# One ring for the probability tiles, a new order of attention's steps, and more decode steps inside the last heads

## The chip, the cores and the metric

The program runs on one core of a Trainium2 chip. The metric is device time in microseconds (us), median over runs of the whole program. TensorE (PE) does the matrix products, VectorE (DVE), ScalarE (ACT) and GpSimd (POOL) the element-wise work, and SyncE (SP) issues all DMA transfers.

## The reference

Sixteen heads of attention, then two feed-forward layers on their output, all checked at float32 accuracy:

```python
q_pool = q.reshape(B, H, S // 2, 2, D).mean(axis=3)          # B, H, S, D = 2, 8, 1152, 64
scores = scale * q_pool @ k.T;  scores -= scores.max(-1)     # per head: 576 queries x 1152 keys
attn = exp(scores) / (exp(scores).sum(-1) + 1e-9)
x = (attn @ v) -> (1152, 512)
x = ((x @ w_a) * (x @ w_b)) @ w_out                          # 512 -> 1536 -> 512, weights in float64
out = sum over 4 experts of p_e * (relu(x @ w1_e) @ w2_e)    # 512 -> 1024 -> 512
```

## The kernel before

Every float32 product is built from rounded parts ("hi" and "lo"), so most operands are first split by a cast on ScalarE and a difference on VectorE or GpSimd.

**Attention.** A head's scores come in nine tiles of 128 keys by 576 queries (a "qk": four matmuls, lines 570 and 575), each followed by an exponential on ScalarE (line 580) into a probability tile e. Each tile is used by a value product (pv, line 656) and, for the sum of each row, by VectorE adds (ad, line 593; on GpSimd for head 1) and products with ones (on, lines 612 and 600). The maximum of each row is needed ahead of the scores: maximum matmuls (mx, line 452) with a VectorE reduction each (lines 467 and 490), then a small transpose (rm) and a DMA into row 64 of QL (row_put). Heads go in pairs; while one pair's scores run, the next pair's Q and K are loaded, split and placed by DMAs (da, dh, dl) and casts (db). A finished pair is normalized: nr, nb (reciprocal of the sums and its spread), two n (product, split into X). Head 0 runs apart, in two parts of its queries (tokens A and C for scores, a and c for value products, x and y for maxima of heads 0 and 1).

**The order** of all of it is written out by hand as lists of such tokens. The loop at line 863 walks through them and issues what each stands for on its engine's queue; each engine runs its queue in order and waits by semaphores. FIRST is for heads 0 and 1, PROG1 for heads 2 and 3, PROG for each pair of heads 4 to 13, PROGZ for 14 and 15. A token that isn't ready may be skipped.

**Probability tiles** are 640 columns wide, eleven of them in a pool (NE = 11); ring() asserts that what lay in a place has been used up. Head 0's half tiles use 512 or 640 of the columns, the others 576.

**Gate and output products.** Weights of the first feed-forward layer come as float64. One gate block f (of 12) has 1 MB of them, loaded into one of two raw tiles (token sd, w_dma) and decoded by w_split_steps into WA, 1024 columns in two chunks of 512. decode64 does a chunk in seven stages with a stop (yield) behind each of the first six: copy on ScalarE (line 198), clamp, shift, or, cast to hi on ScalarE with a mask on VectorE (lines 216, 217), product, then lo (lines 230 and 231, with a subtraction on GpSimd, line 226). A token w runs the decode to its next stop:

```python
        def early_steps():
            yield from w_split_steps(late=False)
            yield from w_split_steps(0, 2 * pools["n"])
```

That is all of block 0's weights (WA0, 13 stops with the one at its end) and the first chunk of block 1's (WA1, 6 stops). What is left of it when attention has been issued is run behind the last pair's normalization, and then the third load:

```python
        for _ in early:
            pass
        while nxt["dma"] < 3:
            w_dma()
```

Then come block 0, whose products are ordered by tokens (first tokens 0 to 383 for all kc, then the others for kc 0 to 2, then kc 3, where the last pair's result lies), WA1's second chunk, blocks 1 to 11 with 72 matmuls each (line 1056), the weights of f + 1 being decoded beside block f, the output product (three groups of 108 in line 1056, the fourth in line 1280) and the experts (lines 1331 and 1403).

Of the kernel before, what the change touches and what calls it, by code (L numbers as in the profile page):

```python
# [7 lines left out]
F32 = mybir.dt.float32  # L8
# [9 lines left out]
SQ = S // 2  # L18
HQ = SQ // 2
KT = S // 128  # L20
# [15 lines left out]
KR = 3  # L36
KN = S // KR
WARM = (8, 4, 3)
NE = 11
NS = 4  # L40
CHAINS = ((0, 1, 2, 3), (4, 5, 6, 7), (8,))
QQ = HQ // 2
# [2 lines left out]
C1 = SQ - C0  # L45
FIRST = """
A
A x wu x
A x x x
A kh1 x  # L50
A x a qh1 a x kl1 a a a x r1 a dh1
C zq
C a c
C c c ql1 qs da1 qh k lv1 lq c klo0 y y
C y y ql y
C qb y lk0 a y y a y E1 y y dh y y y c y mx db1 c qs c R1 c mx mx c mx mx
qk mx dl mx
qk mx
qk mx mx
qk mx mx  # L60
qk mx mx lk2 E2
qk lk1 klo2 qh ldf mx
qk mx ad pv pv k ad pv mx ad klo1 on ad
qk ad db
qk mx pv pv ad pv mx da pv pv on rm qb
""".split()
FIRST_ONLY = set("A C a c x y r1 R1 E1 E2 qh1 kh1 kl1 ql1 da1 dh1 db1 lv1 zq wu".split())
PROG1 = """
on dh mx dn lq pv rw evac
qk  # L70
qk mx ad
qk pv
qk da mx klo0 dl ldf ad nr klo1
qk
qk nb pv mx
qk lk0 pv ad
qk ad mx
qk pv on ad db pv pv ql ad
qk mx
qk ad  # L80
qk on qs pv on qh
qk mx pv ad ad pv sd lk1 evac dn
qk
qk mx ad pv lk2 klo2 pv
qk mx
qk k da pv dl pv pv pv on pv qb n ad dh rm ad
qk db ldf n
""".split()
PROG = """
da klo0 mx pv klo2 pv on sd on pv dn evac  # L90
qk
qk mx
qk
qk pv dl ad ql pv mx
qk
qk dh ad pv pv klo1 rw lk0 lk2 ad mx db lk1 nr
qk ad pv lq ldf pv on mx ad
qk pv ad
qk
qk mx  # L100
qk pv on ad on dh mx dn
qk
qk pv evac qs ad qh
qk mx ad
qk ad pv pv pv k
qk nb mx pv dl db pv on pv da qb n rm
qk ad
qk n ad ldf
""".split()
PROGZ = """  # L110
pv rw pv da db
qk
qk on on ad pv w dn evac nr
qk w
qk pv pv pv
qk ad
qk pv pv ad dh w w
qk dl ad
qk pv w
qk  # L120
qk ad pv ad
qk
qk pv
qk
qk ad on w ad w ad on on
qk
qk pv nb ad ldf ad evac
qk n ad
qk dn n
""".split()  # L130
ENG = {"add1": "P", "klo1": "P", "ql1": "P", "qs1": "P", "klo2": "P", "ql2": "P", "qs2": "P", "add": "V", "qs": "V", "qh": "A", "k": "A", "ql": "V", "klo": "V", "mult": "V", "xhi": "A", "xlo": "V"}
F64_SCALE = 2.0 ** -112
# [4 lines left out]
def kernel(  # L137
# [118 lines left out]
    with tc.manual_schedule():  # L256
        att = ExitStack()
# [1 line left out]
        pair_p = att.enter_context(tc.tile_pool(name="pair", bufs=2))  # L259
        lo_p = att.enter_context(tc.tile_pool(name="lo", bufs=2))  # L260
        b_p = att.enter_context(tc.tile_pool(name="b", bufs=1))
        e_p = att.enter_context(tc.tile_pool(name="e", bufs=NE))
        m_p = att.enter_context(tc.tile_pool(name="m", bufs=2))
        u_p = att.enter_context(tc.tile_pool(name="u", bufs=2))
        r_p = att.enter_context(tc.tile_pool(name="r", bufs=1))
# [6 lines left out]
        pools["tmp"] = lambda i: [tmp_p.tile([128, 256], F32, tag=f"{x}{i}", name=x) for x in "vct"]  # L272
        ps_p = ctx.enter_context(tc.tile_pool(name="ps", bufs=1, space=PSUM))
        PS = ps_p.tile([128, 8, BANK], F32, name="PS")
        turn = {"s": 0, "mx": 0, "st": 0, "ps": 0, "po": 0}

        def psum(kind, base, n, count):
            i = turn[kind]
            turn[kind] = (i + 1) % count
            return PS[:, base + i * n:base + (i + 1) * n, :]  # L280
# [13 lines left out]
        def rows(i):  # L294
            return slice(64 * i, 64 * i + 64)
# [23 lines left out]
        E_t, U_t, D_t = ({} for _ in range(3))  # L319
# [214 lines left out]
        def qk_half(c, u):  # L534
            st = psum("st", 4, 2, 2)
            n, at = ((C0, 0), (C1, C0))[c]
            cs = slice(at, at + n)
            ts = [t for t in (2 * u, 2 * u + 1) if t < KT]
            for j, t in enumerate(ts):
                ks = slice(t * 128, (t + 1) * 128)  # L540
                nc.tensor.matmul(out=st[:, j, :n], lhsT=At[0][:, ks], rhs=QHt[0][:, cs], start=True, stop=False)
                nc.tensor.matmul(out=st[:, j, :n], lhsT=Bt[0][:, ks], rhs=QLt[0][:, cs], start=False, stop=True)
            e = e_p.tile([128, 2, C1], F32, tag="e", name="e")
            k = len(ts)
            nc.scalar.activation(out=e[:, :k, :n], in_=st[:, :k, :n], func=AF.Exp, scale=1.0 / 16.0)
            for j, t in enumerate(ts):
                halves_t[c, t] = e[:, j, :n]
# [8 lines left out]
        def evac_half(c):  # L556
# [5 lines left out]
            if c == 1:  # L562
                den_gather(0, 0, U_t[0][64:65])

        def qk(h, t):
            i = h % 2
            st = psum("st", 4, 2, 2)
            ks = slice(t * 128, (t + 1) * 128)
            for c in range(2):
                nc.tensor.matmul(  # L570
                    out=st[:, c, :HQ], lhsT=At[i][:, ks], rhs=QHt[i][:, c * HQ:(c + 1) * HQ],
                    start=True, stop=False,
                )
            for c in range(2):
                nc.tensor.matmul(  # L575
                    out=st[:, c, :HQ], lhsT=Bt[i][:, ks], rhs=QLt[i][:, c * HQ:(c + 1) * HQ],
                    start=False, stop=True,
                )
            e = E_t[h, t] = e_p.tile([128, 2, C1], F32, tag="e", name="e")[:, :, :HQ]
            nc.scalar.activation(out=e, in_=st[:, :, :HQ], func=AF.Exp, scale=1.0 / 16.0)  # L580

        S_t = {}
# [35 lines left out]
        e_ring = []  # L618

        def ring(new):  # L620
            if len(e_ring) >= NE:
                kind, a, t = e_ring[-NE]
                if kind == "half":
                    assert (a, t) not in halves_t and (a, t + 1) not in halves_t
                else:
                    assert kind == "full" and pv_at[0] > a * KT + t
                    c = [t in x for x in CHAINS].index(True)
                    if len(CHAINS[c]) > 1:
                        assert ad_at[0] > (a, ADDS.index((c, max(1, CHAINS[c].index(t)))))
                    else:  # L630
                        assert on_at[0] > (a, c)
            e_ring.append(new)

        def den(h):
            pr, o = divmod(h, 2)
            if pr == NH // 2 - 1:
                if o == 0:
                    ring(("D", 0, 0))
                    D_t[pr] = e_p.tile([128, 2, C1], F32, tag="e", name="e")[:, :, :HQ]
                for c in range(2):  # L640
                    nc.scalar.activation(
                        out=D_t[pr][rows(o), c, :], in_=PS[rows(c), 1, :HQ], func=AF.Copy, bias=1e-9
                    )
                return
            d = dn_p.tile([128, QQ], F32, tag="dn", name="dn")
            nc.scalar.activation(out=d, in_=PS[:, 0, HQ:HQ + QQ], func=AF.Copy)
            if o == 0:
                dc_t[pr] = m_p.tile([128, SQ // 64], F32, tag="dc", name="dc")
            nc.sync.dma_start(
                out=dc_t[pr][rows(o), :],  # L650
                in_=d.rearrange("(g r) n -> g r n", g=4)[:, 0, :].rearrange("g (p n) -> g p n", p=16),
            )
# [18 lines left out]
        def den_gather(pr, o, den):  # L671
            if o == 0:
                dc_t[pr] = m_p.tile([128, SQ // 64], F32, tag="dc", name="dc")
            nc.sync.dma_start(
                out=dc_t[pr][rows(o), :],
                in_=den.rearrange("o c n -> o (c n)").rearrange("o (p n) -> o p n", p=64),
            )
# [129 lines left out]
        def first(tok):  # L807
# [3 lines left out]
            if tok in "AC":  # L811
                assert tok == "A" or "r1" in emitted
                qk_half(tok == "C", n)
                emitted.update((tok, t) for t in (2 * n, 2 * n + 1))
                if tok == "C" and n == KT // 2:
# [47 lines left out]
        for h in range(1, min(NHX, NH)):  # L863
            s = -1
# [3 lines left out]
            half = ([i for i, t in enumerate(prog) if t == "qk"] + [0] * KT)[KT]  # L868
            for tok in prog if h == 1 else prog[half:] if h % 2 else prog[:half]:
# [8 lines left out]
                elif tok == "qk":  # L878
                    s += 1
                    assert ("row", h) in emitted and all((x, h) in emitted for x in "abhl")  # L880
                    if h == 1:
                        assert {"ql1", "db1", "da1", "dh1"} <= emitted
                    qk(h, s)
                    emitted.add(("qk", h, s))
                elif tok == "mx":
# [4 lines left out]
                elif tok == "rm":  # L890
                    if h + 1 < NH:
                        p = h // 2 + 1
# [9 lines left out]
                elif tok == "pv":  # L902
                    hh, j = divmod(pv_at[0], KT)
# [12 lines left out]
                elif tok == "ad":  # L916
                    hh, j = ad_at[0]
# [5 lines left out]
                elif tok == "on":  # L923
                    hh, j = on_at[0]
# [18 lines left out]
                elif tok in ("nr", "nb", "n"):  # L943
                    i = norm_at[0]
                    pr, i = divmod(i, 4)
# [12 lines left out]
                elif tok in ("lq", "lk0", "lk1", "lk2"):  # L958
                    p = nxt_ld[tok]
                    if p < NH // 2:  # L960
# [4 lines left out]
                        else:  # L965
                            r = int(tok[2])
# [12 lines left out]
                elif tok in ("da", "db", "dh", "dl"):  # L979
                    g = puts[tok[1]]  # L980
                    if g < NH and h > 0:
                        puts[tok[1]] += 1
                        p = g // 2
# [5 lines left out]
                elif tok in ("k", "qs", "qh", "qb"):  # L989
                    p = nxt_pre[tok]  # L990
# [48 lines left out]
        pr = NH // 2 - 1  # L1039
# [62 lines left out]
        w = W.pop(("ab", 0))  # L1102
# [22 lines left out]
        for f in range(1, NF):  # L1125
            if f == STOP:
                return
            w = W.pop(("ab", f))
# [26 lines left out]
        def o_w(d, hf):  # L1155
            while ("o", (d, hf)) not in W:
                next(ahead, None)
            w = W.pop(("o", (d, hf)))
            if d < KC - 1:
                for _ in range(9):  # L1160
                    if nxt["split"] < 15 + 2 * d + hf or splits[14 + 2 * d + hf][:2] not in W:
                        next(ahead, None)
                if (d, hf) == (KC - 2, 1):
                    for _ in ahead:
                        pass
            return w
# [64 lines left out]
        for d in range(KC - 1):  # L1231
            px2 = psum("ps", 0, NTC, 2)
            for hf in range(2):
                w = o_w(d, hf)
# [37 lines left out]
        w = [o_w(KC - 1, hf) for hf in range(2)]  # L1272
# [105 lines left out]
        for k in range(NP // 2):  # L1378
            e = k // 2
# [18 lines left out]
            for tt_i in (5, 6, 7, 8, 0, 1, 2, 3, 4):  # L1398
                po = psum("po", 6, 1, 2)[:, 0, :]
# [63 lines left out]
```

## Time and profile before

| | us |
|---|---|
| median of 3 runs | 864.03 (862.67 to 864.32) |
| the profiled execution | 862.54 |
| its span, first to last instruction | 860.7 |
| TensorE busy | 843.1 |
| VectorE busy | 638.1 |
| ScalarE busy | 338.4 |

The span is what the profile's rows cover; some 1.8 us lie around it. An engine's busy time counts its instructions' time; matmuls are pipelined and their ends are modelled, so a busy TensorE is not one at its peak.

### The profile page before, as it was taken

Reading aid. Unit: us, or ns where it says so; the run is one execution under the profiler, and the core shown is the slowest. Engines: PE = TensorE matmul, PEld = TensorE weight load, DVE = VectorE, ACT = ScalarE, POOL = GpSimd, SP = SyncE. Lnnn points to the kernel's source line nnn. Section 1 sums busy time; section 2 is a strip of 40 time slices with the busy share of each in tenths; the row PEclk is TensorE's granted clock in tenths of the full one; section 3 lists DMA queues with packets and bytes.
Section 4 is the critical chain, followed back from the end, with each engine's and each line's share of the span. In section 5 each row is a group of like instructions: output and inputs, shape, how many; then the busy total and the mean of one; then the engine's idle time right before and its main releaser. Section 6 shows DMA issues by size and latency. Waiting matters only on the chain.

```text
span 860.7 us, 14110 instructions
## 1 busy us (share of the span) xinstructions
PE 843.1 (98%) x5817; PEld 732.8 (85%) x5817; DVE 638.1 (74%) x986; ACT 338.4 (39%) x535; POOL 90.1 (10%) x59
## 2 busy tenths in 40 slices
PE   8999999999969999999999999999999999999998
PEld 6666676667649999999999999989898989899896
DVE  5778888898668778877897885758677675757572
ACT  5556656765743333433323432313232232213130
POOL 6540000000002122212222000000000000000000
PEclk9999999999989999999999999999999999999999
DMA  6357755644402222122232111111111011111002
GB/s 154 95 142 204 178 165 126 171 138 112 102 21 95 82 99 98 49 86 75 74 110 99 50 49 49 50 49 49 49 49 49 5 46 50 50 50 49 1 13 97
DMA packets 24393, 70.66 MB, mean 82 GB/s; under 512 B 6533, under 2 KB 10121, under 8 KB 20745
## 3 DMA queue, kind: packets, MB, share of 16 engines
q1 hardware_dynamic: 24328, 69.76, 26.7%
q8 instruction: 45, 0.74, 0.3%
q14 instruction: 20, 0.16, 0.1%
HBM read 51.96 MB, written 2.39 MB: 63 GB/s over the span
## 4 chain that ended last, share of the span: by engine, by line
PE 93%; DVE 2%; DMA 2%; ACT 1%; issue 1%; SPq 0%; POOL 0%; DVEq 0%; ACTq 0%
PE PS L1056 24%; PE PS L1403 23%; PE PS L1331 21%; PE PS L656 8%; PE PS L570 5%; PE PS L452 4%; PE PS L575 4%; PE PS L1280 2%; DMA VF<-in_vo_dram 1%; PE PS L551 1%; PE PS L612 1%; DMA QL<-mr 1%; DVE R L1042 0%; ACT e L580 0%; PE PS L600 0%
## 5 line engine op out<-in xcount | busy, mean ns | idle before, releaser
L1056 PE MATMUL PS<-X,WA 128*128 128x384 f32 x864 | 152.8, 338 | 7.6 <-ACT WA L216 6.1
L1056 PEld LDWEIGHTS PS<-X,WA 128*128 128x128 f32 x864 | 151.6, 190 | 8.8 <-ACT WA L216 6.4
L1403 PE MATMUL PS<-GT 128*128 128x512 f32 x594 | 139.8, 389 | 0.0
L1403 PEld LDWEIGHTS PS<-GT 128*128 128x128 f32 x594 | 111.2, 188 | 22.8
L1146 DVE TENSOR_TENSOR v<-v,PS 128x576 f32<-128x576 f32 x112 | 82.7, 752 | 42.0 <-PE PS L1331 40.6
L580 ACT ACTIVATE e<-PS 128x576 f32<-128x576 f32 x135 | 83.1, 649 | 51.5 <-PE PS L575 50.8
L1143 ACT ACTIVATE GT<-v 128x576 fp32r<-128x576 f32 (+1 forms) x78 | 52.5, 674 | 118.5 <-DVE v L1146 118.2
L490 DVE TENSOR_REDUCE mc<-PS 128x1 fp32r<-128x1152 f32 x58 | 78.6, 1356 | 21.7 <-PE PS L452 21.0
L1412 DVE SCALAR_TENSOR_TENSOR acc<-PS,p_n,acc 128x512 f32<-128x512 f32 x63 | 47.2, 750 | 58.1 <-PE PS L1403 58.1
L656 PE MATMUL PS<-e,VF 128*32 128x288 f32 x1080 | 81.5, 412 | 0.5 <-ACT U L667 0.3
L1331 PE MATMUL PS<-X,GT 128*128 128x288 f32 x468 | 66.1, 296 | 0.0
L226 POOL TENSOR_TENSOR tmp<-tmp,WA 128x512 f32<-128x512 f32 (+2 forms) x19 | 50.3, 2646 | 150.1 <-DVE tmp L217 136.5
L1403 PE MATMUL PS<-WA,GT 128*128 128x512 f32 x270 | 65.8, 389 | 0.0
L1331 PE MATMUL PS<-GT 128*128 128x288 f32 x456 | 64.5, 296 | 0.0
L1331 PEld LDWEIGHTS PS<-X,GT 128*128 128x128 f32 x468 | 63.8, 189 | 0.2
L570 PE MATMUL PS<-QH,A 128*128 128x288 f32 x270 | 62.5, 313 | 1.2 <-ACT e L580 1.1
L1331 PEld LDWEIGHTS PS<-GT 128*128 128x128 f32 x456 | 62.1, 189 | 0.0
L570 PEld LDWEIGHTS PS<-QH,A 128*128 128x128 f32 x270 | 43.7, 188 | 19.7 <-ACT e L580 10.3
L1403 PEld LDWEIGHTS PS<-WA,GT 128*128 128x128 f32 x270 | 50.6, 188 | 10.4
L1342 DVE SCALAR_TENSOR_TENSOR GT<-v,GT 128x576 fp32r<-128x576 f32 x64 | 48.4, 756 | 13.7 <-ACT GT L1143 12.0
L575 PE MATMUL PS<-QL,B 128*128 128x288 f32 x270 | 57.4, 294 | 0.0
L1056 PE MATMUL PS<-GT,WA 128*128 128x384 f32 x324 | 56.3, 334 | 0.0
(163 smaller groups left out, 1127.7 us busy)
## 6 DMA issues: line engine op xcount, KB each, us to landing
stg<-in_w_dram SPq DMA_DIRECT2D x16, 1024.0 KB
stg<-in_wab_dram SPq DMA_DIRECT2D x12, 1024.0 KB
stg<-in_wout_dram SPq DMA_DIRECT2D x8, 768.0 KB
VF<-in_vo_dram SPq DMA_DIRECT2D x16, 288.0 KB
A<-kl SPq DMA_DIRECT2D x15, 288.0 KB
q<-in_kq_dram SPq DMA_DIRECT2D x7, 576.0 KB
kq<-in_kq_dram SPq DMA_DIRECT2D x21, 192.0 KB
QH<-qh SPq DMA_DIRECT2D x28, 144.0 KB
```

The costliest lines, as they stand in the source:

```text
L226: nc.gpsimd.tensor_tensor(out=t, in0=v, in1=h.bitcast(F32), op=ALU.subtract)
L490: nc.vector.tensor_reduce(out=mc_t[p][:, qi:qi + 1], in_=PS[:, 1:1 + KR, :KN], axis=AX.XY, op=ALU.max)
L570: nc.tensor.matmul(out=st[:, c, :HQ], lhsT=At[i][:, ks], rhs=QHt[i][:, c * HQ:(c + 1) * HQ], start=True, stop=False,)
L575: nc.tensor.matmul(out=st[:, c, :HQ], lhsT=Bt[i][:, ks], rhs=QLt[i][:, c * HQ:(c + 1) * HQ], start=False, stop=True,)
L580: nc.scalar.activation(out=e, in_=st[:, :, :HQ], func=AF.Exp, scale=1.0 / 16.0)
L656: nc.tensor.matmul(out=PS[32 * g:32 * g + 32, 0, :HQ], lhsT=v_of(h)[:, t, g % 2 * 32:g % 2 * 32 + 32], rhs=E_t[h, t][:, g // 2, :], start= ...
L1056: nc.tensor.matmul(out=ps[n], lhsT=wt(kc)[:, wi, w0:w0 + 128], rhs=src(kc)[:, xi, n * TOK:(n + 1) * TOK], start=(kc == first and i == 0), ...
L1143: nc.scalar.activation(out=out, in_=in_, func=func)
L1146: nc.vector.tensor_tensor(out=out, in0=in0, in1=in1, op=op)
L1331: nc.tensor.matmul(out=q[:, n], lhsT=lhs[:, wi, i * 128:(i + 1) * 128], rhs=rhs[:, xi, n * HC:(n + 1) * HC], start=(i == 0 and j == 0), st ...
L1342: nc.vector.scalar_tensor_tensor(out=hv(hs[f][:, 1, ts]), in0=src, scalar=0.0, in1=hv(f32(hs[f][:, 0, ts])), op0=ALU.max, op1=ALU.subtract,)
L1403: nc.tensor.matmul(out=po, lhsT=hs[f][:, hi, ts], rhs=w2s[f // 2][:, f % 2, wi], start=(f == 0 and i == 0), stop=(f == 3 and i == 2),)
```

## The change

The probability tiles become one tensor of twelve places of 576 columns; a half tile of head 0 takes 640 columns from its own start, and ring() checks overlaps by columns. The four lists get another order. In PROGZ there are 19 tokens w instead of 7. In FIRST there are three idle matmuls (wu) instead of one. The token sd moves within PROG1 (head 3 to head 2) and PROG (head 4 to head 5).

```diff
-NE = 11
+NE = 12
 FIRST = """
 A
-A x wu x
-A x x x
-A kh1 x
-A x a qh1 a x kl1 a a a x r1 a dh1
-C zq
+A x x zq
+A qh1 x
+A x kh1 kl1 dh1 x
+A x x wu x a wu x a a r1 da1 a wu
 C a c
-C c c ql1 qs da1 qh k lv1 lq c klo0 y y
-C y y ql y
-C qb y lk0 a y y a y E1 y y dh y y y c y mx db1 c qs c R1 c mx mx c mx mx
-qk mx dl mx
-qk mx
+C k a qs c
+C c c y lk0 qh y
+C y klo0 y y a y y c y y ql1 c y ql qb y a y y y
+C y db1 c a lq lv1 lk2 klo1 R1 c mx mx klo2 qs c mx mx
 qk mx mx
...
 PROG = """
-da klo0 mx pv klo2 pv on sd on pv dn evac
+db lq ad mx pv pv on da rw pv on
+qk dh mx dn
 qk
+qk pv ad mx evac lk0 lk1
+qk ad dl pv pv ad
+qk mx nr ldf
+qk
+qk ad pv klo0 mx pv pv klo2 ad pv
+qk
+qk ad mx
+qk
+qk lk2 ad on ql on on nb mx
+qk qs
+qk pv sd ad pv pv evac ad dn qh
+qk mx dh
+qk pv k klo1 n dl
 qk mx
...
+qk ad pv pv da on ad qb pv pv rm
+qk ad db ldf n
 """.split()
 PROGZ = """
-pv rw pv da db
+w rw w da pv pv on pv on dn w
 qk
-qk on on ad pv w dn evac nr
-qk w
-qk pv pv pv
-qk ad
-qk pv pv ad dh w w
-qk dl ad
-qk pv w
+qk pv ad evac
 qk
-qk ad pv ad
+qk pv w w w db dl
+qk
+qk pv pv w ad pv ad pv
+qk w w dh w
+qk ad on ad
+qk
+qk pv
+qk w ad w w
+qk on ad ldf nr on
 qk
 qk pv
 qk
-qk ad on w ad w ad on on
+qk ad w nb w ad pv w pv ad w evac w ad
 qk
-qk pv nb ad ldf ad evac
-qk n ad
-qk dn n
+qk w dn ad n n
 """.split()
...
-        e_p = att.enter_context(tc.tile_pool(name="e", bufs=NE))
+        e_all = att.enter_context(tc.tile_pool(name="e", bufs=1)).tile([128, NE * SQ], F32, name="e")
...
-            e = e_p.tile([128, 2, C1], F32, tag="e", name="e")
+            at = (KT // 2 + 1) * c + u
+            e = e_all[:, 2 * C1 * at:2 * C1 * (at + 1)].rearrange("p (j n) -> p j n", j=2)
...
+        def e_new():
+            at = turn["e"] % NE
+            turn["e"] += 1
+            return e_all[:, at * SQ:(at + 1) * SQ].rearrange("p (c n) -> p c n", c=2)
...
-            e = E_t[h, t] = e_p.tile([128, 2, C1], F32, tag="e", name="e")[:, :, :HQ]
+            e = E_t[h, t] = e_new()
```

## Rows read from the trace of the kernel before

**Rows 1.** The page: busy time by engine, and the chain that ended last.

```profile
PE 843.1 (98%) x5817; PEld 732.8 (85%) x5817; DVE 638.1 (74%) x986; ACT 338.4 (39%) x535; POOL 90.1 (10%) x59
...
PE 93%; DVE 2%; DMA 2%; ACT 1%; issue 1%; SPq 0%; POOL 0%; DVEq 0%; ACTq 0%
```

**Rows 2.** Busy time by stage: start:end, length, engines, granted clock, DMA.

```profile
0.00:52.60 52.60, 48.08 (x284) 32.70 (x288) 33.06 (x62) 28.38 (x45) 35.31 (x37) 1.00 0.45 123
...
111.69:139.79 28.10, 27.88 (x293) 19.47 (x293) 24.80 (x32) 18.96 (x32) 0.00 (x0) 1.00 0.55 150
...
219.24:246.16 26.92, 26.60 (x281) 16.25 (x281) 15.91 (x32) 18.48 (x37) 0.75 (x1) 1.00 0.30 73
246.16:257.10 10.94, 3.39 (x19) 2.56 (x15) 9.63 (x19) 2.80 (x8) 1.73 (x1) 0.71 0.06 12
257.10:462.70 205.60, 205.60 (x1176) 205.60 (x1177) 167.00 (x304) 71.58 (x112) 52.01 (x20) 0.99 0.26 89
```

**Rows 3.** TensorE's waits: total us, times, longest.

```profile
PE PS L1056 <- ACT WA L216: 6.1, 1, 6.1
PE PS L1056 <- DVE WA L231: 1.5, 1, 1.5
...
PE PS L570 <- ACT e L580: 1.1, 5, 0.2
```

**Rows 4.** The chain that ended last, 215 to 262 us: start, us, what.

```profile
239.99 4.02 PE PS L656 x64
...
246.09 1.96 DVE R L1042
...
252.95 0.41 DVE c L201 x2
...
255.50 0.35 DVE t L230
255.88 1.18 DVE WA L231 x2
257.05 0.04 issue
257.10 5.02 PE PS L1056 x17
```

**Rows 5.** Busy time and granted clock in 2 us of block 0.

```profile
258.00:260.00 2.00, 2.00 (x8) 2.00 (x7) 2.00 (x9) 0.75 (x2) 0.52 (x1) 0.50 0.81 340
```

**Rows 6.** Line 1056 alone: PE and PEld busy, count, granted clock.

```profile
262.00:462.70 200.70, 200.66 (x1158) 200.34 (x1156) 1.00 0.25 86
```

**Rows 7.** Timeline behind block 0: its last gate product, WA2's last step.

```profile
269.33 0.95 DVE L1094 TENSOR_TENSOR asb<-asb,PS 128x768 f32<-128x768 f32 x1 [2.15 <-PE PS L1056]
...
277.94 2.27 DVE L231 TENSOR_TENSOR WA<-tmp 128x512 fp32r<-128x512 f32 x2
```

**Rows 8.** ScalarE's groups by line, 217 to 257 us (two chunks).

```profile
L198 ACT ACTIVATE c<-stg 128x256 f32<-128x256 f32 x4 | 1.6, 442 | 0.9 <-DVE WA L231 0.9
L216 ACT ACTIVATE WA<-v 128x256 fp32r<-128x256 f32 x4 | 1.5, 418 | 1.7 <-DVE v L211 1.7
```

**Rows 9.** Timeline of the last pair: adds, and GpSimd's subtraction.

```profile
226.26 1.61 DVE L593 TENSOR_TENSOR s<-s,e 128x576 f32<-128x576 f32 x2
...
229.94 2.19 DVE L593 TENSOR_TENSOR s<-s,e 128x576 f32<-128x576 f32 x2
...
230.77 0.75 POOL L226 TENSOR_TENSOR t<-v,WA 128x256 f32<-128x256 f32 x1 [177.93 <-ACT WA L216]
```

**Rows 10.** Timeline of the first stage: cast, maxima, their row.

```profile
16.18 1.16 ACT L314 ACTIVATE A<-kq 64x1152 fp32r<-64x1152 f32 x1 [1.69 <-DMA kq<-in_kq_dram]
...
17.10 0.53 PE L452 MATMUL PS<-A,QH 128*64 128x384 f32 x1
...
18.33 0.40 PE L514 MATMUL PS<-nid,mc 128*1 128x128 f32 x3 [0.71 <-DVE mc L481]
...
18.77 0.43 ACT L518 ACTIVATE QL<-PS 1x320 fp32r<-1x320 f32 x1 [0.31 <-PE PS L514]
```

**Rows 11.** VectorE's timeline, 14 to 34 us: reductions for head 1.

```profile
24.15 7.52 DVE L467 TENSOR_REDUCE m<-PS 128x1 f32<-128x384 f32 x14 [5.76 <-PE PS L452]
```

More of the change, by code (lines that the diff above doesn't have):

```diff
@@ L47 @@
 A
-A x wu x
-A x x x
-A kh1 x
-A x a qh1 a x kl1 a a a x r1 a dh1
-C zq
-C a c
-C c c ql1 qs da1 qh k lv1 lq c klo0 y y
-C y y ql y
-C qb y lk0 a y y a y E1 y y dh y y y c y mx db1 c qs c R1 c mx mx c mx mx
-qk mx dl mx
-qk mx
+A x x zq
+A qh1 x
+A x kh1 kl1 dh1 x
+A x x wu x a wu x a a r1 da1 a wu
+C a c
+C k a qs c
+C c c y lk0 qh y
+C y klo0 y y a y y c y y ql1 c y ql qb y a y y y
+C y db1 c a lq lv1 lk2 klo1 R1 c mx mx klo2 qs c mx mx
 qk mx mx
+qk lk1 qh E1 mx mx
 qk mx mx
[L61 to L65, printed above, removed]
+qk da mx
+qk mx ldf mx E2 ad k
+qk mx mx
+qk mx pv ad dh pv ad pv mx pv pv pv mx
+qk on ad
+qk mx pv ad dl ad pv on rm qb on db
 """.split()
@@ L68 @@
 PROG1 = """
-on dh mx dn lq pv rw evac
+da mx dn pv dl lk0 db dh
 qk
-qk mx ad
-qk pv
-qk da mx klo0 dl ldf ad nr klo1
-qk
[L75 to L79, printed above, removed]
-qk ad
-qk on qs pv on qh
-qk mx pv ad ad pv sd lk1 evac dn
-qk
[L84 to L87, printed above, removed]
+qk klo0 lk2 mx evac
+qk rw
+qk pv ad mx ad pv ad pv lk1
+qk mx ldf
+qk nr pv
+qk ad
+qk lq mx
+qk sd ql ad ad dh
+qk klo1 pv on mx
+qk
+qk on qs
+qk mx qh ad
+qk k
+qk nb on klo2 pv ad
+qk mx pv dl pv pv ad dn ad evac mx
+qk ldf db pv on pv pv n ad pv pv n da qb pv rm
+qk
 """.split()
 PROG = """
-da klo0 mx pv klo2 pv on sd on pv dn evac
-qk
-qk mx
[L93 to L108, printed above, removed]
+db lq ad mx pv pv on da rw pv on
+qk dh mx dn
+qk
+qk pv ad mx evac lk0 lk1
[11 more added lines that the diff above has]
+qk pv k klo1 n dl
+qk mx
+qk ad pv pv da on ad qb pv pv rm
+qk ad db ldf n
 """.split()
 PROGZ = """
-pv rw pv da db
+w rw w da pv pv on pv on dn w
 qk
-qk on on ad pv w dn evac nr
-qk w
-qk pv pv pv
-qk ad
-qk pv pv ad dh w w
-qk dl ad
-qk pv w
-qk
-qk ad pv ad
+qk pv ad evac
+qk
+qk pv w w w db dl
[7 more added lines that the diff above has]
+qk on ad ldf nr on
 qk
@@ L274 @@
         PS = ps_p.tile([128, 8, BANK], F32, name="PS")
-        turn = {"s": 0, "mx": 0, "st": 0, "ps": 0, "po": 0}
+        turn = {"s": 0, "mx": 0, "st": 0, "ps": 0, "po": 0, "e": 0}
         def psum(kind, base, n, count):
@@ L620, in ring @@
         def ring(new):
-            if len(e_ring) >= NE:
-                kind, a, t = e_ring[-NE]
+            if new[0] == "half":
+                at = (KT // 2 + 1) * new[1] + new[2] // 2
+                lo, hi = 2 * C1 * at, 2 * C1 * (at + 1)
+            else:
+                lo = turn["e"] % NE * SQ
+                hi = lo + SQ
+            assert hi <= NE * SQ
+            for old in e_ring[:]:
+                (kind, a, t), l, r = old
+                if l >= hi or r <= lo:
+                    continue
                 if kind == "half":
@@ L631, in ring @@
                         assert on_at[0] > (a, c)
-            e_ring.append(new)
+                e_ring.remove(old)
+            e_ring.append((new, lo, hi))
         def den(h):
@@ L638, in den @@
                     ring(("D", 0, 0))
-                    D_t[pr] = e_p.tile([128, 2, C1], F32, tag="e", name="e")[:, :, :HQ]
+                    D_t[pr] = e_new()
                 for c in range(2):
```

## The prediction

> **What bounds the kernel now.** I read the page first: TensorE is busy 98% of the span and the chain that ended last is 93% TensorE [rows 1]. A share that high hides where the rest lies, so the next view is the table by stage. The reader is to see three kinds of stage in it [rows 2]. From 257.10 us on TensorE has no idle time: 205.60 of 205.60 us in the gate and output products. The pair of heads from 111.69 us is nearly as full, 27.88 of 28.10, with VectorE at 24.80. Two stretches are not full: the first 52.60 us (48.08 busy) and the 10.94 us from 246.16 to 257.10 (3.39 busy), where attention hands over to the gate products. The list of TensorE's waits names the same place: 6.1 us for ScalarE's line 216 and 1.5 us for VectorE's line 231, both in line 1056 [rows 3]. Those lines decode float64 weights.
>
> The chain through that stretch says why [rows 4]. Attention ends with value and sum products; behind them VectorE runs the reciprocals and products of the last pair, 246.09 to 252.95, and only then, in its queue order, the steps for the second half of the first gate weight WA0, 252.95 to 257.06: 4.1 us for one chunk of 512 columns. TensorE goes on at 257.10. The loss does not end there: the granted clock is still 0.50 in 258 to 260, the 1.2 GHz level, after TensorE had stood nearly idle [rows 5]; from 262.00 on it is 1.00 [rows 6].
>
> **The change part by part.**
>
> *Decode steps in the last pair.* Old PROGZ has 7 tokens w, so 7 of the 19 stops of the decode run inside attention and the rest is run by the loop behind the final normalization. New PROGZ has 19: both chunks of WA0 and all of the first chunk of WA1 but its last two operations. Gate block 0 then finds WA0 complete when attention ends. Its first 24 matmuls need tokens 0 to 383, its next 36 the chunks of heads of kc 0 to 2; the last pair (kc 3, upper tokens) is first needed at matmul 61. So the normalization, 6.9 us from 246.09 to 252.95 [rows 4], must hide behind 60 matmuls. One costs 200.66 us / 1158 = 0.1733 us [rows 6]; 60 are 10.4 us. It is covered with 3.5 us to spare; without that cover each further us would be a us of TensorE.
>
> What this is worth: from 246.16 to 262.00 are 15.84 us, in which 30 of the 1188 matmuls of line 1056 were done (the code has 12 blocks of 72 and 3 output groups of 108; 1158 lie behind 262.00, up to two of them counted across the border) [rows 6]. At 0.1733 us they take 5.2 to 5.5 us. **Term 1: -10.4 us.** The bounds are -10.6 and, if the clock's part were not given back, the stretch of 10.94 us [rows 2] less the 14 matmuls done in it (2.4 us), -8.5.
>
> What is late next: block 1 needs WA1's second half, still decoded behind the normalization: about 252.95 plus a rest of 1.5 and 4.1 us, 258.6, wanted at matmul 109, 246.16 + 18.7 = 264.9. Block 2 needs WA2, whose decode follows block 0's gate in ScalarE's and VectorE's queues: from the gate's product at 269.33 to the last step's end at 280.21 are 10.9 us [rows 7], against 72 matmuls (12.5 us) of block 1. That slack of 1.6 us moves along with TensorE and stays. Its load, the third, waits for WA0's raw tile; that comes free inside attention now, so SP can issue it before the gate products begin.
>
> *What the steps cost where they go.* On VectorE the last pair is 15.91 us busy of 26.92 [rows 2]. Added are a chunk of 4.1 us and one without its last two operations, 4.1 - 1.5 = 2.6 [rows 4]: 22.6. On ScalarE two chunks more are two times the copies and the conversions, (1.6 + 1.5) / 2 = 1.55 us each [rows 8], on 18.48: 21.6. Both have room by the sum. By the order less so: the conversion (w17) stands before the last two exponentials of head 15 and waits for three VectorE steps with three adds among them, and the sum product after qk 15.2 waits for an add behind two decode steps. Queued behind them are exponentials, and TensorE's scores wait for those two banks later. Bounds: nothing, if the nine products left for the end cover it; 3.7 us, if the last exponentials come after those three of a chunk's seven steps (about 1.5 of the 4.1 us [rows 4]) and three adds (2.2 to 2.4, at half of 1.61 each [rows 9]). I take **Term 2: +1.2 us**, nearer the lower end, because TensorE has 64 records of value products, 4.02 us, to run before it needs the last add [rows 4].
>
> GpSimd takes part in each chunk with one subtraction, so there are two more inside attention. When one ran there, at 230.77, the two VectorE adds beside it took 2.19 us against 1.61 for the pair before [rows 9]: 0.6 us each, which raises VectorE to 23.8 us of 26.92, the share of a steady pair (24.80 of 28.10) [rows 2]. The Trainium skill's page "GPSIMD Engine Reference" (section Key points) says that GpSimd shares its path to SBUF with VectorE and that VectorE instructions with two SBUF inputs contend with it. By that rule of the Trainium skill every add that overlaps pays, Term 2 would be about 2 us, an estimate, the time 854.5, and rival 1 below nearer.
>
> *The first stage.* Old FIRST puts the last maximum matmul of head 0 behind five value products: it starts at 17.10 and the row of maxima at 18.33, and the exponentials of the second query part follow [rows 10]. New FIRST has it behind one. The next limit is ScalarE: its cast of K for head 1 waits for a transfer until 16.18 and takes 1.16, to 17.34, then one exponential; so the row can be copied about 17.7 instead of 18.77 [rows 10]. But two value products move behind that point, and the maxima of head 1 are paced by VectorE, 14 reductions in 7.52 us [rows 11], with one fewer of the next pair's beside them (0.54). Moved DMAs: the load of V for head 1 now stands behind a K and a Q load on SP, but SP runs ahead of TensorE there and the tile is first read after qk 1.6. Two more idle matmuls of 512 columns stand where TensorE waits for these reductions; uncovered they cost 0.46. **Term 3: -0.5 us**, bounds -1.1 (the whole row) and +1.5 (the idle matmuls 0.46, the lost reduction 0.54, and as much again for one that comes late).
>
> *Lists of the other pairs and the ring.* Counting tokens, a pair has the same products and nine runs of narrow matmuls by either list, so TensorE's own work stays at 28.1 us. What can go are the five waits for exponentials, 1.1 us in all [rows 3]; what can come are such waits elsewhere. **Term 4: -0.6 us**, bounds -1.1 and +2.4 (two waits of 0.2 in each of six pairs). Moving the second float64 load from head 4 to head 5 changes only when DMA engines are busy. A ring of twelve places of 576 columns instead of eleven of 640 costs nothing: a place is reused one score later, and what hides the writing is that exponentials wait for TensorE's scores, not for a place; if that cover went, Term 4's upper bound holds it.
>
> Sum: -10.4 + 1.2 - 0.5 - 0.6 = -10.3. The profiled execution took 862.54 us, span 860.7 and 1.8 around it; it becomes 852.2. The median shown is 864.03, 1.5 above it; I predict on the median: 853.7.
>
> **The rivals.** (1) *The crowded last pair becomes the bound.* Steps and adds share VectorE in order at 88%; Term 2 goes to 4.5 or more: 857.0. For it: two-input adds slow beside GpSimd [rows 9]. Against: the steady pairs run at that share with TensorE full [rows 2]. (2) *The gap moves on.* Something behind attention (normalization, WA1, WA2) is late and TensorE waits in block 0, 1 or 2. The thinnest cover is WA2's 1.6 us [rows 7]; a wait of 3 to 5 us there, with the clock falling again, gives about 858. Against: that slack goes with TensorE. (3) *Slower: the new pair list stalls.* The maximum products use three banks that one reduction must clear; if a reduction stands behind an add or a K difference, TensorE waits. The lists repeat, so it comes six times. It decides from 1.7 us a pair (10.3 / 6); at 2 us: 853.7 + 12 = 866. Against: VectorE keeps 3.3 us of a pair idle [rows 2].
>
> **How the numbers follow.** Forecast 0.70, rival 1 0.14, rival 2 0.10, rival 3 0.06. A measurement here tells 0.2% (1.7 us) from no change. The first three all lie well below 862.3, so faster is 0.92, with 0.02 for same where rival 2 and rival 3 shade into it; slower 0.06. The bounds of the four terms give -12.8 to -0.9; all four at one end is unlikely. Range: 850.5, all lower bounds and a low median, to 859.0, which takes in rivals 1 and 2.
>
> **What would show it.** Right: no wait in line 1056 before matmul 61; granted clock 1.00 from 240 to 270; the stretch from attention's last product to 1188 matmuls later about 206 us; the pair stages 28.1 us; the last pair 27 to 29 us; VectorE there about 23 us. The prediction is wrong if TensorE waits for line 216, 231 or 314 in block 0, if head 15's last exponentials come over 3 us behind their scores, or if every pair from 111 us on is longer than before.

## The result, and the profile after

The changed kernel takes 850.46 us (median of 4 runs, 850.15 to 850.90), the kernel before 863.65 in the same session: a ratio of 0.9849, 95% interval 0.9831 to 0.9866. That is 13.2 us less where 10.3 were forecast: faster, as expected, and at the very edge of the range, whose lower end was 850.5. The profiled execution spans 848.4 us, 12.3 less than the 860.7 of before.

The page of the changed kernel, busy time and the chain that ended last, to be read against [rows 1]:

```profile
PE 839.8 (99%) x5819; PEld 731.9 (86%) x5819; DVE 637.8 (75%) x986; ACT 336.4 (40%) x535; POOL 91.2 (11%) x59
...
PE 92%; ACT 2%; DMA 2%; DVE 1%; issue 1%; POOL 0%; SPq 0%; ACTq 0%; DVEq 0%
```

VectorE and ScalarE have done the same work in 0.3 and 2.0 us less; the change is one of place. Where, the table by stage shows (columns as in [rows 2]):

```profile
0.00:52.90 52.90, 48.96 (x286) 32.96 (x290) 33.29 (x62) 28.36 (x46) 33.75 (x36) 1.00 0.45 122
...
108.48:136.17 27.69, 27.60 (x297) 19.70 (x293) 24.83 (x31) 18.77 (x32) 0.00 (x0) 1.00 0.56 151
...
218.78:244.12 25.34, 25.13 (x249) 15.24 (x249) 21.08 (x53) 19.01 (x40) 4.89 (x3) 1.00 0.41 115
244.12:450.40 206.28, 206.28 (x1194) 206.28 (x1191) 169.37 (x300) 72.19 (x114) 50.72 (x19) 1.00 0.24 84
450.40:848.40 398.00, 394.21 (x2352) 360.00 (x2350) 267.53 (x392) 107.09 (x157) 0.00 (x0) 1.00 0.13 45
```

The stretch of 10.94 us with 3.39 us of products is gone: 206.28 of 206.28 us are busy from attention's end on, at a granted clock of 1.00, where before 216.54 (10.94 + 205.60) passed. From the last gate or output product of line 1072 (before: 1056) to the end it is 398.4 us in both kernels. A pair of heads takes 27.69 instead of 28.10.

TensorE's waits, the first two and two more of nine (compare [rows 3]):

```profile
PE PS L756 <- DVE X L762: 1.5, 1, 1.5
PE PS L514 <- DVE mc L481: 0.5, 1, 0.5
...
PE PS L576 <- DMA A<-kl: 0.2, 1, 0.2
PE PS L606 <- ACT e L657: 0.2, 1, 0.2
```

No wait for a weight is left (the gate products are line 1072 now). The chain at attention's end goes through the decode steps, now inside attention (compare [rows 4]):

```profile
239.16 0.76 ACT WA L216 x2
239.93 0.01 issue
239.94 1.19 ACT e L586 x2
...
241.89 1.68 PE PS L606 x12
243.56 0.62 PE PS L672 x8
244.19 17.88 PE PS L1072 x102
```

TensorE's own rows of the same stretch, with the last scores' low part first:

```profile
237.24 0.43 PE L581 MATMUL PS<-QL,B 128*128 128x288 f32 x2
237.59 4.09 PE L672 MATMUL PS<-e,VF 128*32 128x288 f32 x64
241.89 1.19 PE L606 MATMUL PS<-VF,ones 128*64 128x288 f32 x8 [0.21 <-ACT e L657]
```

The reader is to see that the conversion of a weight (line 216) does stand ahead of the last two exponentials, as the prediction had it: the last one starts 2.8 us behind the end of its scores (240.49 and 237.66). It costs next to nothing all the same, because TensorE meanwhile runs its 64 records of value products, 4.09 us, and then waits 0.2 us, for a copy that stands behind those exponentials on ScalarE.

I add the lengths by equal work. Head 2's first score starts at 53.11 before and at 53.40 after; attention ends at 246.16 and 244.12. So the first stage is 0.3 us longer, head 2 to attention's end 2.3 shorter (193.05 and 190.72), the handover 10.3 shorter: 12.3 in all. The 2.3 us have two parts: head 2 to head 12, the lists of the pairs, 2.7 shorter (140.81 and 138.09), and head 12 to attention's end, where PROGZ begins, 0.4 longer (52.24 and 52.63).

### The profile page after: what moved, and what is told of

Same layout as the page of the kernel before. It is cut to its first block, busy times and chain, and to the rows that moved or that the text cites. A ratio compares the mean times of both kernels' runs of the same rounds, so it can differ in the third digit from the quotient of the medians.

```text
span 848.4 us, 14130 instructions
## 1 busy us (share of the span) xinstructions
PE 839.8 (99%) x5819; PEld 731.9 (86%) x5819; DVE 637.8 (75%) x986; ACT 336.4 (40%) x535; POOL 91.2 (11%) x59
## 4 chain that ended last, share of the span: by engine, by line
PE 92%; ACT 2%; DMA 2%; DVE 1%; issue 1%; POOL 0%; SPq 0%; ACTq 0%; DVEq 0%
PE PS L1072 24%; PE PS L1419 23%; PE PS L1347 21%; PE PS L672 7%; PE PS L452 4%; PE PS L576 4%; PE PS L581 3%; PE PS L1296 2%; PE PS L618 1%; PE PS L552 1%; DMA stg<-in_wab_dram 1%; ACT e L586 1%; DMA A<-kl 1%; DMA q<-in_kq_dram 0%; PE PS L606 0%
## 5 line engine op out<-in xcount | busy, mean ns | idle before, releaser
L1072 PEld LDWEIGHTS PS<-X,WA 128*128 128x128 f32 x864 | 149.7, 188 | 0.5 <-issue 0.5
L1072 PE MATMUL PS<-X,WA 128*128 128x384 f32 x864 | 150.0, 334 | 0.0
L1419 PEld LDWEIGHTS PS<-WA,GT 128*128 128x128 f32 x270 | 50.6, 188 | 10.4
```

The source lines that it names most:

```text
L1072: nc.tensor.matmul(out=ps[n], lhsT=wt(kc)[:, wi, w0:w0 + 128], rhs=src(kc)[:, xi, n * TOK:(n + 1) * TOK], start=(kc == first and i == 0), ...
L1419: nc.tensor.matmul(out=po, lhsT=hs[f][:, hi, ts], rhs=w2s[f // 2][:, f % 2, wi], start=(f == 0 and i == 0), stop=(f == 3 and i == 2),)
```

## The experiments

Lengths named below run from head 2's first score to the first gate product ("attention's end"), and from pair to pair by the first score of each even head. In different executions with the old first list (with or without one more `on`), head 2 started at 52.97 to 54.62 us, so spans of single profiles are not compared.

**The decode steps alone (progz_alone).** The old FIRST, PROG1 and PROG, with the new ring and PROGZ:

```diff
 FIRST, PROG1, PROG: as before
-PROGZ: 7 tokens w
+PROGZ: 19 tokens w, and the rest of the new list
```

> The kernel before with the new ring and the new PROGZ (19 decode steps) and nothing else. Theory (the handover is the gain of the decode steps; the pair lists gain about 3 us by themselves): about -9.5 us, 854.2; block 0 starts without a wait and the granted clock stays at 1.00; pairs of heads stay at 28.1 us. Rival (the handover needs the earlier lists as well, the last pair becomes the bound without them): 857 or more, with TensorE waiting in the last pair.

Measured: 852.81 us, ratio 0.9877 (0.9862 to 0.9891), 10.5 us faster. The stage that answers to the 216.54 us of before:

```profile
246.30:452.60 206.30, 206.30 (x1194) 206.28 (x1191) 169.39 (x300) 72.22 (x114) 50.72 (x19) 1.00 0.24 84
```

Head 2 to attention's end is 193.27 us, 0.2 more than before, though 12 more steps are in it. Head 12 to attention's end, the part that the new list changes, is 52.67 us instead of 52.24; four other profiles with the old PROGZ have 52.23 to 52.29. So the whole gain of the handover comes from the steps, and the new list with its crowding costs 0.4 us.

**The same by taking them away (seven_steps).**

```diff
 PROGZ of the changed kernel
-19 tokens w
+the first 7 of them
```

> The changed kernel with only the first 7 of PROGZ's 19 decode tokens; the rest is decoded behind attention as before. Theory (decode steps give 10.3 us at the handover and cost 0.8 in the last pair): 860.0, with the wait for line 216 and the fall of the clock back. Rival (the crowded last pair costs about 3 us, hidden in the sum): 857.8 or less.

Measured: 861.40, ratio 0.9976 (0.9967 to 0.9986): about 11 us above the changed kernel. The waits of before are back to the tenth:

```profile
PE PS L1072 <- ACT WA L216: 6.1, 1, 6.1
PE PS L1072 <- DVE WA L231: 1.5, 1, 1.5
```

The rival is out. Head 2 to attention's end is 190.99 us, not shorter than with 19 steps (190.72). In this execution one wait for a transfer was 0.6 us longer, so the 12 steps cost some 0.3 us.

**How much of it is the clock (gap_filled).** In the kernel before:

```diff
             for i in range(2):
                 mm3(*ab[i], kcs, ncs, 0, KC - 1)
+                if i == 0 and len(ncs) == 1:
+                    warm(30)
```

> The kernel before with 30 idle matmuls of 512 columns behind the first 12 matmuls of block 0, where TensorE waits for WA0; they write a bank that is not read again. Theory (of the 10.4 us of the handover about 2 are the clock that falls in the gap): -2.1 us, 861.5, granted clock 1.00 through the gap. Rival (the clock's part is no loss because TensorE waits for later weights instead): 863.6 with a new wait in block 1 or 2.

Measured: 861.23, ratio 0.9980 (0.9972 to 0.9989), 1.7 to 1.9 us faster. From the first gate product to the last one of line 1056 it is 214.40 us, before 216.17: 1.8 less. The gap in stretches of 4 us:

```profile
250.00:254.00 4.00, 4.00 (x19) 3.27 (x19) 3.28 (x5) 0.53 (x2) 0.00 (x0) 1.00 0.00 0
254.00:258.00 4.00, 2.72 (x13) 2.01 (x11) 3.96 (x13) 0.75 (x2) 1.73 (x1) 1.00 0.21 31
258.00:262.00 4.00, 3.90 (x22) 3.90 (x23) 3.43 (x13) 1.51 (x4) 1.50 (x1) 1.00 0.56 231
```

The granted clock is 1.00 throughout, where before it was 0.50 at 258 to 260 [rows 5]. TensorE still waits for line 231 (1.4 us), and behind it for no later weight; so about 1.8 of the 10.3 us of the handover were the clock.

**The ring (old_pool).** The new lists with `NE = 11` and the old pool of tiles:

> The changed kernel's four lists with the old pool of eleven probability tiles of 640 columns. Theory (the ring gives nothing, exponentials never wait for a place): 850.5, within 0.5. Rival (the twelfth place is what lets the pairs run faster): 853 or more, with ScalarE waiting for value products ahead of exponentials and pairs near 28.1 us.

Measured: 850.79, ratio 0.9852 (0.9836 to 0.9868), pairs of 27.72 us: the same. With either, ScalarE's exponentials in attention wait for TensorE's scores and not for a value product, here with the old pool from 82 to 240 us:

```profile
ACT e L580 <- PE PS L575: 44.1, 50, 3.1
```

The ring is worth nothing in time that these runs can tell.

**The first stage (old_first).** The changed kernel with the old FIRST (and one `on` at its end):

> The changed kernel with the old list FIRST (one token on added at its end so that the lists fit). Theory (the new FIRST gains nothing, head 2 starts 0.3 us later with it): 850.2, -0.3. Rival (the new FIRST gains the 0.5 us that were forecast): 851.0.

Measured: 850.73, ratio 0.9860 (0.9846 to 0.9873) beside 0.9849 in another session. Neither theory is told from the other: the difference is 0.3 us by the medians and 0.9 by the ratios, and each ratio's interval is over 1 us wide to either side. What the new FIRST is worth stays open within that.

**The lists of the pairs alone (pairs_alone).** New PROG1 and PROG, old FIRST (with `on` behind it) and old PROGZ (with `pv` ahead of it):

> The kernel before with the new ring and the new PROG1 and PROG; FIRST and PROGZ are the old ones, with one token on behind FIRST and one token pv ahead of PROGZ so that the pieces fit. Theory (the pair lists take out waits of TensorE for weights that the wait list of its matmuls does not show): about -3 us, 860.6, pairs of 27.7 us, the gap in front of block 0 as before. Rival (the pairs are faster only through other parts): 863.6, pairs of 28.1 us.

Measured: 862.13, ratio 0.9991 (0.9982 to 1.0000): 0.8 us or so, not 3. Four pairs of the profile are 27.5 to 27.7 us as the theory said, but one is 29.28, and head 14 starts late. TensorE's waits, and VectorE in the slow pair:

```profile
PE PS L576 <- DMA A<-kl: 1.4, 1, 1.4
PE PS L452 <- DVE mc L490: 1.3, 2, 0.7
```

```profile
119.62 0.17 DVE L698 TENSOR_SCALAR dc<-dc 128x9 f32<-128x9 f32 x1 [1.76 <-DMA dc<-dn]
```

The new lists ask for two transfers earlier than they landed here: the sums of a head (nr behind dn), and the low part of K ahead of head 14, where no maximum product stands in between. Of the new pair lists' gain 2.7 us went back in this execution. It was the slowest of the ten, 864.39 us, so the two waits explain this profile and not the median: why the lists bring less here than in the changed kernel (850.46 against the 852.81 of progz_alone) is not shown. The changed kernel has the second wait too, at 0.2 us. How often the first one strikes was not counted.

**Which wait goes, first try (one_mx_moved).** In the kernel before:

```diff
-qk
-qk mx
+qk mx
+qk
 qk pv on ad on dh mx dn
```

> The kernel before with one token of PROG moved: the maximum product that stood behind the first scores of a pair's second head stands ahead of them (mx | qk instead of qk mx). Theory (the 0.2 to 0.3 us a pair at that place are a wait for an exponential, because four scores followed one another with too little between): five pairs lose about 0.25 us each, 862.4. Rival (the wait is ScalarE's own order and only moves): 863.6, the wait at another qk.

Measured: 862.88, ratio 1.0001 (0.9992 to 1.0009); pairs of 28.10. The theory fell. The wait stands at a pair's third scores, behind another maximum product, just as before:

```profile
139.76 0.68 PE L452 MATMUL PS<-kh,QB 128*128 128x384 f32 x3
140.65 0.53 PE L570 MATMUL PS<-QH,A 128*128 128x288 f32 x2 [0.21 <-ACT e L580]
```

I had named the wrong place. In the kernel before ScalarE's queue at a pair's start reads:

```profile
137.92 0.29 ACT L646 ACTIVATE dn<-PS 128x144 f32<-128x144 f32 x1 [1.74 <-issue]
138.24 0.82 ACT L667 ACTIVATE U<-PS 64x288 f32<-64x288 f32 x2
139.08 1.20 ACT L580 ACTIVATE e<-PS 128x576 f32<-128x576 f32 x2
```

Two copies of the finished head, den and evac, stand ahead of the pair's first exponential, whose scores started at 137.73; the third scores need that exponential's bank.

**That place (copies_later).**

```diff
-da klo0 mx pv klo2 pv on sd on pv dn evac
+da klo0 mx pv klo2 pv on sd on pv
 qk
-qk mx
+qk mx dn evac
```

> The kernel before with one edit in PROG: the copies of the finished head (dn, evac) stand behind the second scores of the next pair instead of ahead of the first. Theory (the 0.27 to 0.37 us a pair that TensorE loses at its third scores are these two copies ahead of the first exponential on ScalarE): five pairs lose about 0.3 us each, pairs of 27.8 us, time 861.7, and no wait for an exponential behind the second maximum. Rival (any order of ScalarE there costs the same, only the list as a whole helps): pairs of 28.1 us.

Measured: 862.47, ratio 0.9996 (0.9987 to 1.0005), pairs of 27.97 (27.94 to 27.98). The wait at the third scores is gone, but a good part of it comes back two scores later, where the value product needs the copied bank:

```profile
140.24 1.16 PE L656 MATMUL PS<-e,VF 128*32 128x288 f32 x14 [0.23 <-ACT U L667]
```

So 0.13 us a pair, not 0.3. The new lists put the value product further behind the copies as well.

**The add (add_first).**

```diff
-qk n ad ldf
+qk ad n ldf
```

> The kernel before with one edit in PROG: a pair's last add stands ahead of the low part of the normalization (xlo) on VectorE, not behind it. Theory (the product with ones waits 0.16 us a pair for that add): pairs of 27.93 us, time 862.4. Rival (the add waits for its exponential anyway): pairs of 28.1 us.

Measured: 862.16, ratio 0.9995 (0.9986 to 1.0003), pairs of 28.00. The profile shows 0.1 us a pair; the time can't tell it.

**The second float64 load (load_moved).**

```diff
-da klo0 mx pv klo2 pv on sd on pv dn evac
+da klo0 mx pv klo2 pv on on pv dn evac
-qk pv evac qs ad qh
+qk pv evac sd qs ad qh
```

> The kernel before with the token of the second float64 load moved from head 4 to head 5, nothing else. Theory (the pair of heads 4 and 5 took 28.74 instead of 28.09 us because that load holds up the load of V): -0.6 us, 863.0, that pair at 28.1 us. Rival (it only moves the crowding into the next loads): 863.6.

Measured: 863.28, ratio 0.9999 (0.9990 to 1.0008). In the profile the pair of heads 4 and 5 is 28.12 us, the length of the others, instead of 28.74:

```profile
82.23:110.35 28.12, 27.91 (x297) 19.49 (x293) 24.99 (x32) 18.94 (x31) 0.00 (x0) 1.00 0.72 201
```

The time does not show it; 0.6 us is inside the interval. Nor is the 0.6 a steady price of the load. With the load left in head 4, that pair is 29.30 us in gap_filled, 28.42 in add_first, 28.21 in one_mx_moved, and no longer than the others in copies_later (the next run):

```profile
81.17:109.11 27.94, 27.74 (x297) 19.55 (x293) 25.09 (x32) 18.83 (x31) 0.00 (x0) 1.00 0.81 201
```

So with the load in head 4 the pair is 0 to 1.2 us longer than its neighbours, by execution; in every profile with the load in head 5 it is level with them. That the load is the cause fits this, but one profile's 0.6 us does not measure it.

**All three (three_edits).** The edits of copies_later, add_first and load_moved together in the kernel before:

> The kernel before with three edits in PROG together: copies later, last add first, second float64 load in head 5. Theory (these three waits are what the new lists of the pairs take away): pairs of 27.65 us, the pair of heads 4 and 5 too; from the start of head 2 to attention's end 190.7 us plus 0.3, instead of 193.0; time 860.9. Rival (the order as a whole counts): pairs stay above 27.8.

Measured: 861.21, ratio 0.9979 (0.9970 to 0.9988), 1.6 to 1.8 us faster. Head 2 to attention's end is 191.08 us, of the 193.05 before and the 190.72 of the change. The pairs:

```profile
80.76:108.51 27.75, 27.55 (x297) 19.50 (x293) 24.33 (x32) 18.84 (x31) 0.00 (x0) 1.00 0.72 201
108.51:136.32 27.81, 27.80 (x296) 19.55 (x292) 24.79 (x32) 18.84 (x31) 0.00 (x0) 1.00 0.57 151
```

From head 2 to head 12 it is 138.99 us: three small edits bring 1.8 of the 2.7 us that the new lists of the pairs bring there, though 0.6 of either is the heads 4 and 5 of the one profile before. In every pair they bring 0.28 us, more than the 0.13 and 0.1 of the two edits that act there: with only one of them another wait partly takes its place. The pairs stop at 27.81, not 27.65, so by its own sign (above 27.8) the rival is not out: what the new lists have beyond that lies in none of the three edits.

**A further step (qh_later).** In the changed kernel:

```diff
-qk pv sd ad pv pv evac ad dn qh
-qk mx dh
+qk pv sd ad pv pv evac ad dn
+qk mx qh dh
```

> The changed kernel with one edit in PROG: the cast of the next pair's Q (qh) stands one score later on ScalarE. Theory (0.17 us a pair is left in the changed kernel where a score waits for an exponential behind that cast): pairs of 27.5 us, time 849.7, faster than both. Rival (the wait moves to the next exponential): pairs of 27.66 us, 850.5.

Measured: 850.03 (849.60 to 850.52), ratio 0.9852 (0.9838 to 0.9865) in its session: level with the change, not shown to be faster. The pairs do come down to 27.52 us. But this execution loses it again at the last boundary:

```profile
108.18:135.70 27.52, 27.52 (x296) 19.69 (x292) 24.73 (x31) 18.78 (x32) 0.00 (x0) 1.00 0.59 153
190.74:218.69 27.95, 27.05 (x294) 19.27 (x290) 23.80 (x33) 16.11 (x30) 0.00 (x0) 1.00 0.47 114
```

```profile
218.69 0.50 PE L576 MATMUL PS<-QH,A 128*128 128x288 f32 x2 [0.91 <-DMA A<-kl]
```

Four pairs gain some 0.16 each, and the wait for head 14's K is 0.9 us instead of 0.2. The edit is not shown to cause that: TensorE is ready for this score 4.9 us after the transfer was issued in both profiles (issued at 212.89 here, at 213.66 in the changed kernel), and can go on 5.8 us after it here, 5.1 there. In the other profiles with the new pair lists it is 5.2 to 5.8. The new lists leave this transfer 4.9 us; the kernel before left it 7.6.

## Why the prediction was right, and where a size was off

**Term 1, the handover (-10.4).** Right in mechanism and size. Stage against stage it is 216.54 - 206.28 = 10.3 us; by progz_alone's time 10.5, by seven_steps' about 11. The covers held as worked out: the normalization ended at 250.92 (0.46 us from 250.46), 6.8 us after attention's end at 244.12, ahead of matmul 61 at 254.6. WA2's last step:

```profile
265.85 2.27 DVE L231 TENSOR_TENSOR WA<-tmp 128x512 fp32r<-128x512 f32 x2
```

It ends at 268.12 and block 2's first matmul, the 145th, starts at 269.19: a slack of 1.1 where 1.6 was forecast, and no wait. (Before, that matmul started at 281.54, 1.3 us behind the 280.21 of [rows 7], so the forecast had the cover too thick by 0.3.) So rival 2 did not come. That a part of the term is the clock, 1.7 to 1.9 us, was shown by gap_filled; the rest is the wait itself.

**Term 2, the crowded last pair (+1.2).** The order is as feared, the price was too high: 0.3 us by seven_steps, 0.4 by progz_alone. The last two exponentials are 2.8 us late, with 7 steps 0.2 (seven_steps), so 2.8 of the feared 3.7 us did come; the sign "over 3 us behind their scores" was missed by little. But the nine value products left for the end hide it, which the prediction had named as the reason for the lower end. VectorE stands at 21.08 us of 25.34 in the last stage without stopping TensorE; about 23 were forecast. Rival 1 falls with it.

**Term 3, the first stage (-0.5).** Neither shown nor refuted: a term of this size is below what old_first can tell, and the profile has +0.3 in a stage that varies by over 1 us between executions.

**Term 4, the lists of the pairs (-0.6).** This is the term that was mis-sized: the profile has -2.7 us from head 2 to head 12 (-2.3 to attention's end, together with Term 2), and -2.4 us is what the changed kernel has over progz_alone (852.81 to 850.46; the new FIRST is in that). My lower bound was -1.1, and the pairs, forecast to stay at 28.1 us, take 27.69. The step that failed is "What can go are the five waits for exponentials, 1.1 us in all": the list of matmul waits [rows 3] is no bound on what an order can give. Three things were not in it. A wait listed at 0.21 us was 0.38 longer than the same step without one (from maximum products to scores 0.90 us, and 0.52 at the same place in copies_later). The product with ones started 1.15 us behind its value products where 0.99 is the step without a wait, an add's lateness that the list puts on the weight load, not on the matmul. And the pair of heads 4 and 5 took 28.74 instead of 28.10, beside the float64 load, whose place I had set at nothing ("changes only when DMA engines are busy"); by load_moved and the other profiles this is 0 to 1.2 us, by execution. The three together, undone in the old lists, give 1.8 of the 2.7 us. What is left, 0.15 us a pair, stays open.

Rival 3 did not come: in the changed kernel no pair stalls on a reduction. In the profile of pairs_alone one did, by 1.3 us, where VectorE had waited for a transfer.

The ring was rightly put at nothing. In the profiles the sum was 2.0 us short (10.3 and 12.3): 2.1 from Term 4 and 0.8 from Term 2, less 0.8 from Term 3 and 0.1 from Term 1. On the medians it was 2.9 us short; the other 0.8 is in the choice of executions, since the kernel before was profiled at 862.54 us with a median of 863.65 and the changed one at 850.15 with 850.46. (The kernel before had medians of 862.83 to 863.30 in the later sessions.) That the time lies at the range's end and not beyond is in part luck: Term 4 left its own bounds, and the other terms did not come at their lower ones.

## What to carry to other kernels

Where two stages hand over, ask what the first product of the next stage needs and which queue makes it: work that does not depend on the end of the first stage belongs ahead of it, even on engines that are nearly full, as long as independent products cover the last steps. A gap can cost more than its wait: here some 1.8 of the 10.3 us were the clock, still at 0.50 behind it [rows 5]. The list of a busy engine's waits is no bound on what a better order can give: compare the start-to-start distance of the same pair of steps with and without a wait, and look at whole pairs, not at single edits, because one wait taken out lets the next one show. Before one profile's stage is given a cause, look at the same stage in other executions: one pair here was 0 to 1.2 us longer with the same order of its loads.

## What the runs showed that I had not expected

GpSimd's subtraction beside VectorE's adds. I had priced it at 0.6 us on VectorE each. In the changed kernel the three of them read:

```profile
223.22 0.74 POOL L226 TENSOR_TENSOR t<-v,WA 128x256 f32<-128x256 f32 x1 [168.47 <-ACT WA L216]
231.73 0.73 POOL L226 TENSOR_TENSOR t<-v,WA 128x256 f32<-128x256 f32 x1 [7.77 <-ACT WA L216]
239.72 3.42 POOL L226 TENSOR_TENSOR t<-v,WA 128x256 f32<-128x256 f32 x1 [7.26 <-ACT WA L216]
```

```profile
223.48 0.77 DVE L230 TENSOR_TENSOR t<-v,WA 128x256 f32<-128x256 f32 x1 [0.17 <-ACT WA L216]
...
239.38 0.49 DVE L217 TENSOR_SCALAR c<-v 128x256 uint32<-128x256 uint32 x2
239.78 0.75 DVE L599 TENSOR_TENSOR VF<-VF,e 128x576 f32<-128x576 f32 x1
240.45 0.76 DVE L222 SCALAR_TENSOR_TENSOR c<-stg,c 128x256 f32<-128x256 uint32 x2
241.12 0.75 DVE L599 TENSOR_TENSOR VF<-VF,e 128x576 f32<-128x576 f32 x1
241.79 0.75 DVE L717 TENSOR_TENSOR U<-U,R 128x576 f32<-128x576 f32 x1
```

At 223 the subtraction takes 0.74 us and VectorE's small one beside it 0.77 instead of the 0.42 that the same instruction takes at 250.83, with GpSimd idle. At 239.7 it takes 3.42 us, under a row of VectorE instructions, most of them with two inputs, that keep their 0.75. That row was already running when the subtraction started, and it ends at 242.54; the subtraction ends at 243.14, 0.6 us later, near the 0.73 and 0.74 us of the other two. So it looks as if it had waited for the whole row, which is read from these times and not tested. The Trainium skill's page "GPSIMD Engine Reference" (section Key points) says that the two contend for SBUF with such instructions. The traces agree, and show that either side can be the one that pays, here 0.35 us or 2.7. Spans on GpSimd are rough in these records, so the 3.42 is an order of size. Here it falls on a result that nobody waits for until 250.83.
